# First chunk's loads moved ahead of a branch, weights regrouped on the queue, and one head's mask moved to VectorE, in a kernel of banded attention and two MLPs

## The chip, the cores and the metric

The program runs on one core of a Trainium2 chip. The metric is the device time of one execution in microseconds; for the kernel before it is the median of three runs. A core has TensorE (PE in the rows, with its weight loads as PEld), VectorE (DVE), ScalarE (ACT), GpSimd (POOL) and SyncE (SP), which here issues transfers; each engine takes its instructions in order from its own queue.

## The reference

Attention with sink keys and a window, for 2 batches, 8 heads, 768 positions and 64 columns a head, and then two MLPs on the 1,536 tokens:

```python
scores = q @ k.transpose(0, 1, 3, 2) / sqrt(64)
rel = pos[:, None] - pos[None, :]
keep = (pos[None, :] < n_sink) | ((rel >= 0) & (rel < window))   # 4 sinks, window 128
a = exp(where(keep, scores, -1e9) - rowmax)
attn = (a / (a.sum(-1) + 1e-9)) @ v
x = attn as [1536, 512]
h = x @ w_in;   x = (h - tanh(h)) @ w_out                        # 512 -> 2048 -> 512
h = x @ w_in2;  x = (h * clip(h + 3, 0, 6) / 6) @ w_out2
```

`n_sink`, `window` are 64-bit integers in memory, and the MLPs' weights reach the chip as 64-bit floats.

## The kernel before

**Tiles.** The tokens are cut into three chunks of 512 (`CHUNKS`), each four blocks of 128 queries. The heads are taken in four pairs. For a chunk c and a pair m the attention consists of these steps: `begin` loads the pair's queries and keys (tile `qk`, two transfers a run of blocks, one for each head) and its values (tile `v`, two transfers); `score` (L447) runs for each of the four blocks, for both heads: matmul into a bank `ps_a`, on VectorE a predicated copy (L469) that puts the block's own diagonal half over the earlier one, then one operation that masks, scales and takes the minimum (L471), and on ScalarE an exponential with its sum (L475). `soft` (L479) normalises on VectorE (L492). `turn_sink` and `turn_p` (L504) transpose the probabilities on TensorE; for each head of the pair ScalarE copies them to `p` (L513) and GpSimd makes two masked copies of them, with `affine_select`, one for the block's own keys and one for the keys of the block before (L517, L521). `mix` (L526) multiplies with the values, and splits the result into a high part `xh` (ScalarE, L547) and a low part `xl` (VectorE, L548), the inputs of the MLP.

**The MLP** has 64 groups a chunk (`GROUPS`), each of 12 matmuls of 128x512: every product is done as three (high by high, high by low, low by high: L175, L176, L177). Two groups share one weight tile of 128x1024, called a pair p of groups; 32 weights make the two MLPs. In the first chunk each weight is decoded from its 64-bit form: `w_load` (SP, tile `raw`, 1 MB, four buffers), `w_sign` (ScalarE, two operations, L127 and L129, tile `r`, two buffers), `w_scale` (ScalarE, L107, tile `dec`), `w_exponent` (VectorE, L118), `w_round` (VectorE, L135), `w_keep` (SP, stores the decoded weight for later chunks), and `w_split` into high `wh` (ScalarE for the weights 0 and 1, L151; GpSimd for the others, L149) and low `wl` (VectorE, L152). `w_step(p, half)` calls these for weights up to six ahead of p. The later chunks load the kept weights, and their attention runs between the groups of the chunk before.

**Order.** A few loads, the masks and the test of `n_sink` and `window` (DMA of the two scalars, `scalars_value`, `is_band`) stand ahead of a branch; the banded case is the one that runs. Behind the branch a planner orders the instructions of each engine by a simulated timeline; within what the data allows it may place a later one first. `keep_in_program_order` pins an instruction behind the one before it on its engine; that is done for the loads and the scalings of the weights 0 to 5. `startup` (L779) lists the attention of chunk 0 and drops the twelve calls of `w_step` for p from -6 to -1 into it; the factor 1.25 decides where:

```python
while warm and left < 1.25 * len(warm):
    mlp.w_step(*warm.pop(0))
```

With 41 operations in the list, the first of the twelve calls comes when 14 are left, and the first scaling behind `mix` of pair 1. Ahead of the branch only pair 0 of chunk 0 is loaded, on SP. The tile `vsk` of sink values is set to zero by GpSimd behind the branch (L415), and eight small transfers (`sinks`, L443) follow on SP.

## Time and profile before

| | |
|---|---|
| time of the runs | 671.25 us (671.24, 671.25, 672.27) |
| time of the profiled execution | 676.76 us |
| its span | 675.0 us |
| TensorE busy | 647.0 us, 96% of the span |
| VectorE, ScalarE, GpSimd busy | 394.4, 365.7, 103.8 us |
| mean granted clock of TensorE | 0.978 |
| moved by DMA | 98.87 MB |

Busy shares count the time in which an engine has an instruction under way; matmuls overlap, so that a busy TensorE need not be at its peak pace. The granted clock is a share of 2.4 GHz: 1.00 is the upper level and 0.50 the lower. Times within the execution count from the start of the span. Line numbers are those of the kernel before.

### The profile page before, as it was taken

The numbers are of one execution on the slowest core, as the hardware profiler recorded it, in microseconds if no ns is written. First come the engines' busy times: TensorE is split into PE (matmuls) and PEld (weight loads), VectorE is DVE, ScalarE is ACT, GpSimd is POOL, SyncE is SP. The second block draws the span as 40 slices with busy tenths as digits, with TensorE's granted clock in tenths as the row PEclk, the third lists the DMA queues.
The fourth block names the chain that finished last, engine by engine and source line by source line (L and its number), as shares of the span: only waits on it lengthen the run. The fifth ranks groups of instructions, "written<-read, shape, count | busy, mean of one in ns | idle before, by whom it ended". The sixth has DMA issues, their size and how long they took to land.

```text
span 675.0 us, 8142 instructions
## 1 busy us (share of the span) xinstructions
PE 647.0 (96%) x2924; PEld 494.7 (73%) x2924; DVE 394.4 (58%) x711; ACT 365.7 (54%) x614; POOL 103.8 (15%) x114
## 2 busy tenths in 40 slices
PE   3897899999999999999999999999999999999995
PEld 2555677777777787887776777778788888888884
DVE  4659599887797754365555465444355444455431
ACT  3769779887978633354444454444354443454421
POOL 1234122234452421000102020201000000000000
PEclk9959699999999999999999999999999999999999
DMA  5969879968668731423314221113133323221001
GB/s 104 324 168 340 306 292 312 319 248 304 224 216 293 227 113 33 135 104 125 103 63 125 91 95 63 62 63 126 62 126 124 102 86 115 73 70 55 0 1 67
DMA packets 38896, 98.87 MB, mean 146 GB/s; under 512 B 17856, under 2 KB 25024, under 8 KB 30656
## 3 DMA queue, kind: packets, MB, share of 16 engines
q1 hardware_dynamic: 38848, 98.27, 44.3%
q8 instruction: 25, 0.41, 0.2%
q14 instruction: 23, 0.19, 0.1%
HBM read 78.33 MB, written 19.92 MB: 146 GB/s over the span
## 4 chain that ended last, share of the span: by engine, by line
PE 90%; ACT 2%; DVE 2%; DMA 2%; SPq 2%; POOL 1%; issue 1%; POOLq 0%; DVEq 0%; ACTq 0%
PE ps_h L175 13%; PE ps_y L175 13%; PE ps_h L176 13%; PE ps_h L177 13%; PE ps_y L176 13%; PE ps_y L177 13%; PE ps_a L463 5%; PE ps_a L543 4%; PE ps_a L511 1%; DMA raw<-in_w_dram 1%; SPq L282 1%; ACT r L127 1%; ACT r L129 1%; DVE dec L118 1%; DMA raw<-in_window_dram 1%
## 5 line engine op out<-in xcount | busy, mean ns | idle before, releaser
L176 PE MATMUL ps_y<-gl,wh 128*128 128x512 f32 x384 | 151.0, 394 | 0.0
L177 PE MATMUL ps_y<-gh,wl 128*128 128x512 f32 x384 | 150.0, 391 | 0.0
L175 PE MATMUL ps_y<-gh,wh 128*128 128x512 f32 x384 | 143.9, 400 | 0.0
L152 DVE TENSOR_TENSOR wl<-raw,wh 128x1024 fp32r<-128x1024 f32 x64 | 79.3, 1239 | 58.2 <-ACT wh L151 57.3
L151 ACT CAST wh<-raw 128x1024 fp32r<-128x1024 f32 x64 | 67.2, 1050 | 48.6 <-PE ps_y L176 40.9
L175 PEld LDWEIGHTS ps_y<-gh,wh 128*128 128x128 f32 x384 | 71.7, 188 | 22.0 <-issue 5.9
L176 PEld LDWEIGHTS ps_y<-gl,wh 128*128 128x128 f32 x384 | 72.1, 188 | 16.6 <-issue 1.9
L177 PEld LDWEIGHTS ps_y<-gh,wl 128*128 128x128 f32 x384 | 72.1, 188 | 15.6 <-issue 0.3
L175 PE MATMUL ps_h<-xh,wh 128*128 128x512 f32 x192 | 77.8, 409 | 1.2 <-ACT xh L547 1.2
L177 PE MATMUL ps_h<-xh,wl 128*128 128x512 f32 x192 | 77.2, 402 | 0.6 <-DVE wl L152 0.6
L176 PE MATMUL ps_h<-xl,wh 128*128 128x512 f32 x192 | 77.1, 402 | 0.0
L175 PE MATMUL ps_h<-yh,wh 128*128 128x512 f32 x192 | 76.6, 402 | 0.0
L176 PE MATMUL ps_h<-yl,wh 128*128 128x512 f32 x192 | 76.2, 397 | 0.0
L177 PE MATMUL ps_h<-yh,wl 128*128 128x512 f32 x192 | 76.0, 396 | 0.0
L233 ACT ACTIVATE th<-ps_h,three 128x512 f32<-128x512 f32 x48 | 32.8, 686 | 70.1 <-PE ps_h L177 69.9
L235 DVE SCALAR_TENSOR_TENSOR th<-th,ps_h 128x512 f32<-128x512 f32 x48 | 32.8, 684 | 53.3 <-ACT th L233 53.1
L463 PE MATMUL ps_a<-qk 64*128 64x264 f32 (+1 forms) x192 | 48.4, 477 | 11.4 <-DVE keep L709 6.8
L475 ACT ACTIVATE sc<-sc,mn 128x132 f32<-128x132 f32 x96 | 38.3, 401 | 37.1 <-DVE mn L471 36.9
L149 POOL CAST wh<-dec 128x1024 fp32r<-128x1024 f32 x30 | 37.5, 1250 | 114.6 <-PE ps_y L176 68.1
L227 ACT ACTIVATE th<-ps_h 128x512 f32<-128x512 f32 x48 | 28.6, 597 | 48.9 <-PE ps_h L177 39.4
L229 DVE TENSOR_TENSOR th<-ps_h,th 128x512 f32<-128x512 f32 x48 | 32.9, 686 | 36.2 <-ACT th L227 36.2
L463 PEld LDWEIGHTS ps_a<-qk 64*128 64x128 f32 x192 | 23.6, 220 | 32.6 <-issue 20.6
(74 smaller groups left out, 903.8 us busy)
## 6 DMA issues: line engine op xcount, KB each, us to landing
raw<-in_w_dram SPq DMA_DIRECT2D x32, 1024.0 KB
raw<-keep SPq DMA_DIRECT2D x32, 1024.0 KB
keep<-dec SPq DMA_DIRECT2D x32, 512.0 KB
out_dram<-ob SPq DMA_DIRECT2D x12, 256.0 KB
qk<-in_qkv_dram SPq DMA_DIRECT2D x8, 325.0 KB
qk<-in_qkv_dram SPq DMA_DIRECT2D x8, 260.0 KB
qk<-in_qkv_dram SPq DMA_DIRECT2D x8, 195.0 KB
v<-in_qkv_dram SPq DMA_DIRECT2D x8, 160.0 KB
```

The costliest lines, as they stand in the source:

```text
L149: nc.gpsimd.tensor_copy(out=wh, in_=src)
L151: nc.scalar.copy(out=wh, in_=src)
L152: nc.vector.tensor_sub(out=wl, in0=src, in1=wh.bitcast(F32))
L175: mm(out=ps, lhsT=wh, rhs=ah, start=first, stop=False)
L176: mm(out=ps, lhsT=wh, rhs=al, start=False, stop=False)
L177: mm(out=ps, lhsT=wl, rhs=ah, start=False, stop=last)
L227: nc.scalar.activation(out=th, in_=ps, func=ACTF.Tanh)
L229: nc.vector.tensor_sub(out=u, in0=ps, in1=th)
L233: nc.scalar.activation(out=th, in_=ps, func=ACTF.Relu, bias=self.three)
L235: nc.vector.scalar_tensor_tensor(out=u, in0=th, scalar=6.0, in1=ps, op0=ALU.min, op1=ALU.mult)
L463: nc.tensor.matmul(out=ps[:, 0:w], lhsT=qk[:, e, 0:128], rhs=qk[:, first:e + 1, 128:KEYS], start=True, stop=True)
L475: nc.scalar.activation(out=sc, in_=sc, func=ACTF.Exp, scale=-1.0, bias=mn, accum_out=s["sm"][:, a, i:i + 1])
```

## The change

- The queries and keys of the pairs 0 to 2 of chunk 0 are loaded ahead of the branch by SP, and the values of all four pairs by ScalarE's queue. The buffers for them are fixed tiles (three for `qk`, used in turn by m; four for `v`, one for each m) that the later chunks use too. Pair 3's queries and keys go into the tile of pair 0, once its scores are done; `begin` of pair 3 stands at tick 4 instead of 6.
- In the list of `startup`, `w_load(0)` comes right behind `begin` of pair 0, and `w_load(1)` to `w_load(3)` directly behind `begin` of pair 3, pinned in that order. `w_load` does nothing for a weight already loaded.
- The factor 1.25 becomes 0.8: the first of the twelve calls comes when nine operations are left, and the first scaling behind the last `score` of pair 3.
- For the second head of a pair in chunk 0, VectorE makes the two masked copies directly out of the PSUM bank, by multiplying with masks of zeros and ones; ScalarE's copy and GpSimd's two selections of that head go. Two more mask tiles are made for it ahead of the branch.
- GpSimd clears `vsk` ahead of the branch. The high parts of the weights 0 and 1 are made by GpSimd, as those of the others.
- The other arm of the branch, which does not run here, takes its room from the same tiles.

```diff
@@ -83,7 +83,7 @@
     def w_load(self, p):
-        if p >= self.n_pairs:
+        if p >= self.n_pairs or p in self.raw:
             return
         nc = self.nc
         if p < PAIRS:
@@ -145,7 +145,7 @@
         src = self.dec.pop(p).bitcast(F32) if p < PAIRS else self.raw.pop(p)
         wh = self.spl_p.tile([128, 1024], F32R, tag="wh", name="wh")
         wl = self.spl_p.tile([128, 1024], F32R, tag="wl", name="wl")
-        if 2 <= p < PAIRS:
+        if p < PAIRS:
             nc.gpsimd.tensor_copy(out=wh, in_=src)
         else:
             nc.scalar.copy(out=wh, in_=src)
@@ -268,25 +268,28 @@
     return out
-def load_pair(nc, qk_p, v_p, qkv, m, rs):
-
-    n = sum(r[3] for r in rs)
-    qk = qk_p.tile([128, n, KEYS], F32, tag="qk", name="qk")
-    v = v_p.tile([128, 2, n, 64], F32, tag="v", name="v")
+def pair_buffers(pool, pairs, n):
+
+    qk = [pool.tile([128, n, KEYS], F32, tag=f"qk{m}", name="qk") for m in range(pairs - 1)]
+    v = [pool.tile([128, 2, n, 64], F32, tag=f"v{m}", name="v") for m in range(pairs)]
+    return qk, v
+
+
+def load_qk(dma, qk, qkv, m, rs):
     for i, b, j, k in rs:
         for a in range(2):
             h = slice(64 * a, 64 * (a + 1))
-            nc.sync.dma_start(out=qk[h, i:i + k, :], in_=qkv[b, 2 * m + a, h, j:j + k, 0:KEYS])
+            dma(out=qk[h, i:i + k, :], in_=qkv[b, 2 * m + a, h, j:j + k, 0:KEYS])
+
+
+def load_v(dma, v, qkv, m, rs):
     for i, b, j, k in rs:
         for a in range(2):
-            nc.sync.dma_start(out=v[:, a, i:i + k, :], in_=qkv[b, 2 * m + a, :, j:j + k, KEYS:BLOCK])
-    return qk, v
-
-
-def load_blocks(nc, pool, qkv, h, runs, first=0, last=BLOCK, tag="raw"):
-    n = sum(r[3] for r in runs)
-    t = pool.tile([128, n, last - first], F32, tag=tag, name=tag)
-    for i, b, j, m in runs:
+            dma(out=v[:, a, i:i + k, :], in_=qkv[b, 2 * m + a, :, j:j + k, KEYS:BLOCK])
+
+
+def load_blocks(nc, t, qkv, h, rs, first, last):
+    for i, b, j, m in rs:
         nc.sync.dma_start(out=t[:, i:i + m, :], in_=qkv[b, h, :, j:j + m, first:last])
     return t
@@ -399,20 +402,19 @@
-    def __init__(self, ctx, tc, qkv, vs, ready, masks, ident, mlp):
+    def __init__(self, ctx, tc, qkv, vs, ready, vsk, masks, ident, mlp):
         self.tc, self.nc = tc, tc.nc
         _, self.H, _, self.NB, _ = qkv.shape
         self.mlp, self.qkv, self.vs, self.ident = mlp, qkv, vs, ident
         self.ready = ready
-        self.own_keep, self.mask = masks
+        self.own_keep, self.mask, self.own, self.prev = masks
         pool = lambda nm, n: ctx.enter_context(tc.tile_pool(name="at_" + nm, bufs=n))
-        self.qk_p, self.v_p, self.s_p = pool("qk", 2), pool("v", 3), pool("s", 2)
+        self.s_p = pool("s", 2)
         self.p_p, self.px_p = pool("p", 2), pool("px", 4)
         self.scale = -1.0 / 64.0 ** 0.5
         self.wide = True
         self.st = {}
-        self.vsk = pool("const", 1).tile([32, self.H // 2, 4, 128], F32, name="vsk")
-        self.nc.gpsimd.memset(self.vsk, 0.0)
+        self.vsk = vsk
     def bank(self, kind):
@@ -429,10 +431,12 @@
         qb = self.query_blocks(c)
         kb = ([(qb[0][0], qb[0][1] - 1)] if qb[0][1] > 0 else []) + qb
         s = self.st[it] = dict(qb=qb, kb=kb)
-        if it == (0, 0):
-            s["qk"], s["v"] = self.ready
-        else:
-            s["qk"], s["v"] = load_pair(self.nc, self.qk_p, self.v_p, self.qkv, m, runs(kb))
+        qk, v = self.ready
+        s["qk"], s["v"] = qk[m % len(qk)], v[m]
+        if c > 0 or m >= len(qk):
+            load_qk(self.nc.sync.dma_start, s["qk"], self.qkv, m, runs(kb))
+        if c > 0:
+            load_v(self.nc.sync.dma_start, s["v"], self.qkv, m, runs(kb))
     def sinks(self, c):
@@ -509,10 +513,17 @@
         pt = self.bank("p")
         for i in range(nq):
             nc.tensor.transpose(pt[:, 128 * i:128 * (i + 1)], s["sc"][:, a, i, 0:128], self.ident)
+        px = self.px_p.tile([128, nq, 2, 128], F32, tag="px", name="px")
+        s["px", a] = px.rearrange("p j t s -> p (j t s)")
+        if self.wide and a == 1:
+            src = pt[:, 0:128 * nq].rearrange("p (j s) -> p j s", s=128)
+            for t, keep in ((1, self.own), (0, self.prev)):
+                nc.vector.tensor_tensor(
+                    out=px[:, :, t, :], in0=src, in1=keep.unsqueeze(1).to_broadcast([128, nq, 128]), op=ALU.mult
+                )
+            return
         p = self.p_p.tile([128, 128 * nq], F32, tag="p", name="p")
         nc.scalar.copy(out=p, in_=pt[:, 0:128 * nq])
-        px = self.px_p.tile([128, nq, 2, 128], F32, tag="px", name="px")
-        s["px", a] = px.rearrange("p j t s -> p (j t s)")
         src = p.rearrange("p (j s) -> p j s", s=128)
         nc.gpsimd.affine_select(
             out=px[:, :, 1, :], in_=src, pattern=[[0, nq], [1, 128]], compare_op=ALU.is_ge,
@@ -554,7 +565,8 @@
         for m in range(self.H // 2):
             it = (c, m)
             at = lambda k, *p: out[2 * m + k].append(p)
-            at(0, self.begin, it)
+
+            out[4 if it == (0, 3) else 2 * m].append((self.begin, it))
             if m == 0:
                 at(1, self.sinks, c)
             for i in range(n):
...
...
@@ -699,8 +715,8 @@
         for c in range(NSINK):
             nc.vector.memset(self.is_sink[:, c:c + 1], float(c))
         self.keep = [tile_(f"keep{j}", SLOT) for j in range(3)]
-        self.wm, self.far = tile_("wm", 1), tile_("far", 128)
-        self.own_keep = tile_("own_keep", 128, I32)
+        self.wm, self.far = tile_("wm", 1), self.keep[2][:, 0:128]
+        self.own_keep = di
     def finish(self, n_sink, window):
         nc, delta, is_sink = self.nc, self.delta, self.is_sink
@@ -718,7 +734,10 @@
         big = 8.0 * BIG
         for keep in self.keep:
             nc.vector.tensor_scalar(out=keep, in0=keep, scalar1=big, scalar2=-big, op0=ALU.mult, op1=ALU.add)
-        return self.own_keep, self.keep
+        own, prev = self.delta, self.past
+        nc.vector.tensor_scalar(out=prev, in0=delta, scalar1=0.0, scalar2=None, op0=ALU.is_gt)
+        nc.vector.tensor_scalar(out=own, in0=delta, scalar1=0.0, scalar2=None, op0=ALU.is_le)
+        return self.own_keep, self.keep, own, prev
 def when(t, n):
@@ -744,13 +763,20 @@
     kf = GROUPS // 4
     glob = ctx.enter_context(tc.tile_pool(name="glob", bufs=1))
     raw = scalars(tc, glob, n_sink, window)
-    ready = load_pair(nc, glob, glob, qkv, 0, [(0, 0, 0, CHUNKS[0] // 128)])
+    vsk_room = glob.tile([128, kd * 4 * 128], F32, name="vsk")
+    vsk = vsk_room[0:32].rearrange("p (m i d) -> p m i d", m=kd, i=4)
+    nc.gpsimd.memset(vsk, 0.0)
+    ready = pair_buffers(glob, kd, 5)
+    for m, qk in enumerate(ready[0]):
+        load_qk(nc.sync.dma_start, qk, qkv, m, [(0, 0, 0, CHUNKS[0] // 128)])
     ident = glob.tile([128, 128], F32, name="ident")
     make_identity(nc, ident)
     masks = Masks(tc, glob)
     warm = glob.tile([128, 1], F32, name="warm")
     nc.vector.memset(warm, 0.0)
     nc.scalar.activation(out=warm, in_=warm, func=ACTF.Exp)
+    for m, v in enumerate(ready[1]):
+        load_v(nc.scalar.dma_start, v, qkv, m, [(0, 0, 0, CHUNKS[0] // 128)])
     ns, win = scalars_value(tc, glob, raw)
     flag = is_band(tc, glob, ns, win)
     kept = masks.finish(ns, win)
@@ -758,12 +784,15 @@
     with tc.If(band != 0) as cmp:
         with ExitStack() as arm:
             mlp = Mlp(arm, tc, w64, out, CHUNKS, kd, kf)
-            at = BandAttention(arm, tc, qkv, vs, ready, kept, ident, mlp)
+            at = BandAttention(arm, tc, qkv, vs, ready, vsk, kept, ident, mlp)
             banded(mlp, at)
     with cmp.Else():
         with ExitStack() as arm:
             mlp = Mlp(arm, tc, w64, out, CHUNKS, kd, kf, ahead=3)
-            at = DenseAttention(arm, tc, qkv, ident, ns, win, mlp)
+
+            flat = [t.rearrange("p j c -> p (j c)") for t in ready[0]]
+            room = [*flat, ready[1][0].rearrange("p a j c -> p (a j c)"), vsk_room, flat[0]]
+            at = DenseAttention(arm, tc, qkv, room, ident, ns, win, mlp)
             dense(mlp, at)
@@ -778,11 +807,13 @@
 def startup(mlp, at):
     first = [p for t in at.ticks(0) for p in t]
+    for n in range(4):
+        first.insert(1 if n == 0 else first.index((at.begin, (0, 3))) + n, (mlp.w_load, n))
     warm = [(p, h) for p in range(-6, 0) for h in range(2)]
     for n, p in enumerate(first):
         p[0](*p[1:])
         left = len(first) - 1 - n
-        while warm and left < 1.25 * len(warm):
+        while warm and left < 0.8 * len(warm):
             mlp.w_step(*warm.pop(0))
```

## Rows read from the trace of the kernel before

**Rows 1.** Page, part 2: busy tenths and granted clock in 40 slices.
```profile
PE   3897899999999999999999999999999999999995
...
PEclk9959699999999999999999999999999999999999
```

**Rows 2.** Windows by stage: busy us of PE, PEld, DVE, ACT, POOL; clock, DMA.
```profile
25.95:55.00 29.05, 25.47 (x115) 15.68 (x114) 18.24 (x57) 23.64 (x48) 6.77 (x11) 0.71 0.78 246
55.00:72.95 17.95, 12.34 (x57) 7.78 (x56) 14.52 (x16) 13.97 (x19) 8.93 (x7) 0.86 0.95 329
72.95:81.40 8.45, 8.45 (x26) 6.75 (x27) 3.83 (x6) 6.64 (x8) 1.04 (x1) 0.70 0.89 300
81.40:668.00 586.60, 585.91 (x2667) 454.26 (x2665) 343.41 (x557) 310.82 (x500) 81.09 (x83) 1.00 0.40 133
```

**Rows 3.** Groups, 0 to 82 us: busy us, mean ns, idle before.
```profile
L129 ACT ACTIVATE r<-raw 128x1024 f16<-128x1024 f32 x9 | 12.1, 1355 | 0.0
...
L135 DVE CUSTOM_DVE_ANT_0 dec<-dec,r 128x2048 uint16<-128x2048 uint16 x8 | 11.3, 1417 | 0.4 <-ACT r L129 0.4
...
L107 ACT ACTIVATE dec<-raw 128x1024 f32<-128x1024 f32 x9 | 10.0, 1141 | 2.4 <-DMA keep<-dec 1.5 <-DVE wl L152 0.9
...
L176 PE MATMUL ps_h<-xl,wh 128*128 128x512 f32 x21 | 9.5, 451 | 0.0
...
L521 POOL TENSOR_SCALAR_AFFINE_SELECT px<-p 128x512 f32<-128x512 f32 x8 | 7.5, 935 | 0.0
...
L152 DVE TENSOR_TENSOR wl<-dec,wh 128x1024 fp32r<-128x1024 f32 x5 | 7.4, 1472 | 0.3 <-ACT wh L151 0.3
...
L118 DVE TENSOR_SCALAR dec<-dec 128x1024 int32<-128x1024 int32 x8 | 5.7, 710 | 1.7 <-ACT dec L107 1.7
...
L548 DVE TENSOR_TENSOR xl<-ps_a,xh 128x512 fp32r<-128x512 f32 x4 | 2.7, 686 | 3.4 <-ACT xh L547 3.4
```

**Rows 4.** Chain of waits of 0 to 82 us: start, length, what.
```profile
19.07 6.86 DMA raw<-in_w_dram
...
25.95 1.19 ACT r L127
...
69.03 3.26 PE ps_a L543 x13
...
81.13 0.23 PE ps_h L175
```

**Rows 5.** Timeline of VectorE and ScalarE: start, length, instruction, idle before it.
```profile
6.20 0.28 DVE L713 TENSOR_SCALAR far<-delta,wm 128x128 f32<-128x128 f32 x1
...
6.85 1.63 DVE L711 CAST own_keep<-keep 128x128 int32<-128x128 f32 x1
...
9.66 0.30 DVE L471 CUSTOM_DVE_ANT_0 sc<-ps_a,keep 128x132 f32<-128x132 f32 x1
...
13.49 0.08 DVE L471 DVE_READ_ACCUMULATOR2_ANT mn<- 128x1 f32 x1
...
15.93 0.30 DVE L471 CUSTOM_DVE_ANT_0 sc<-ps_a,keep 128x132 f32<-128x132 f32 x1 [2.36 <-PE ps_a L463]
...
18.48 1.34 DVE L492 TENSOR_TENSOR sc<-sc,rs 128x512 f32<-128x512 f32 x2
...
55.01 0.39 ACT L475 ACTIVATE sc<-sc,mn 128x132 f32<-128x132 f32 x1
```

**Rows 6.** Timeline of SP's queue: start, time spent issuing, transfers.
```profile
8.42 2.70 SPq L443 DMA_DIRECT2D vsk<-in_vs_dram  x8
...
12.49 1.16 SPq L282 DMA_DIRECT2D v<-in_qkv_dram  x2
```

**Rows 7.** Windows: the first loads, and a stage without late data.
```profile
3.00:6.76 3.76, 0.00 (x0) 0.03 (x1) 1.66 (x12) 0.00 (x0) 0.16 (x1) 1.00 0.85 171
...
18.05:28.62 10.57, 10.57 (x65) 7.48 (x61) 8.30 (x44) 7.58 (x24) 3.31 (x6) 1.00 1.09 328
```

**Rows 8.** Windows, all engines: early in the unbroken stream.
```profile
80.00:120.00 40.00, 40.00 (x170) 29.97 (x169) 37.82 (x61) 34.60 (x54) 8.45 (x7) 1.00 0.87 315
```

More of the change, by code (lines that the diff above doesn't have):

```diff
@@ L573, with __init__ @@
     BUFS = dict(t=1, v=1, s=1)
-    def __init__(self, ctx, tc, qkv, ident, n_sink, window, mlp):
+    def __init__(self, ctx, tc, qkv, room, ident, n_sink, window, mlp):
         super().__init__(ctx, tc, qkv, ident, mlp)
-        self.raw_p = ctx.enter_context(tc.tile_pool(name="at_raw", bufs=1))
         nc, const, S = self.nc, self.const, self.S
+        self.raws = room[3:6]
         self.n_sink = n_sink
-        ki = const.tile([128, S], I32, name="ki")
+        ki, self.kpos, self.rel = (t[:, 0:S] for t in room[0:3])
+        ki = ki.bitcast(I32)
         nc.gpsimd.iota(ki, pattern=[[1, S]], base=0, channel_multiplier=0)
-        self.kpos = const.tile([128, S], F32, name="kpos")
         nc.vector.tensor_copy(out=self.kpos, in_=ki)
         nc.gpsimd.iota(ki, pattern=[[-1, S]], base=0, channel_multiplier=1)
-        self.rel = const.tile([128, S], F32, name="rel")
         nc.vector.tensor_copy(out=self.rel, in_=ki)
@@ L598, in head @@
         s = self.st[it] = dict(h=h, qb=qb, kb=[(b, j) for b in bs for j in range(NB)])
-        s["qr"] = load_blocks(nc, self.raw_p, self.qkv, h, runs(qb), 0, 128, "rawq")
-        kv = load_blocks(nc, self.raw_p, self.qkv, h, runs(s["kb"]), 128, BLOCK)
-        s["kr"], s["vr"] = kv[:, :, 0:SLOT], kv[:, :, SLOT:SLOT + 64]
+        nq, nk = len(qb), len(s["kb"])
+        q, k, v = (
+            t[:, 0:n * w].rearrange("p (j c) -> p j c", c=w)
+            for t, n, w in zip(self.raws, (nq, nk, nk), (128, SLOT, 64))
+        )
+        s["qr"] = load_blocks(nc, q, self.qkv, h, runs(qb), 0, 128)
+        s["kr"] = load_blocks(nc, k, self.qkv, h, runs(s["kb"]), 128, KEYS)
+        s["vr"] = load_blocks(nc, v, self.qkv, h, runs(s["kb"]), KEYS, BLOCK)
         self.split(it, 128)
```

## The prediction

> **What bounds the kernel now.** I read the page first, then the stages, the chain of waits, and the queues. The slices [rows 1] show TensorE full from about 80 us to the end; only the first five slices have gaps and a low granted clock. The stages [rows 2] say it exactly: from 81.40 to 668 us TensorE is busy 585.91 of 586.60 us at clock 1.00, so there nothing but less TensorE work would help, and the change removes none. Before that, TensorE waits for the first chunk's attention. So the question is only how early the unbroken MLP stream can begin.
>
> I measure that with one number, the **zero point**: the time from which all MLP matmuls would have had to run back to back to stand where they stand. By 82 us 21 + 21 + 20 matmuls into ps_h and 3 into ps_y have run (65; the group of L176 stands in [rows 3]). At full clock one takes 0.23 us of the chain [rows 4] (0.232 by the starts of two that lie twelve apart, 78.17 and 80.96). 65 x 0.232 = 15.1 us, so the zero point is 82 - 15.1 = 66.9 us. What the change gains is 66.9 less the new zero point, less any new stall afterwards.
>
> What made it 66.9? In the chain [rows 4] the weights are issued at 19.07 and the first lands 6.86 us later; ScalarE's decoding starts on that landing; much later the last pair's output matmuls run from 69.03 for 3.26 us (the granted clock is 0.86 and 0.70 around them [rows 2], a mixture of the 2.4 and 1.2 GHz levels), then the copy of the output, then the MLP at 72.95. In between, from 25.95 to 55 us, ScalarE is busy 23.64 of 29.05 us and VectorE 18.24 [rows 2]: attention of pairs 2 and 3 and decoding of weights share both in-order queues, and an exponential of pair 3's scores still runs at 55.01 [rows 5].
>
> **The change, part by part.** All terms are built forward to E, the time at which the last pair's attention output is split.
>
> Masks and memset. VectorE starts the scores at 9.66 [rows 5]. Its cast at L711 took 1.63 us beside GpSimd's memset of vsk, the next one as long, both ended at 8.48; L713, a like one without the memset beside it, took 0.28 [rows 5]. With the memset moved ahead, about 1.2 us goes; the two new mask tiles cost 0.28 each at most. Scores start near 9.0 us. Cover: before, the keys of pair 0 were there by 7.73; if the added traffic delays them past 9.0 the gain of 0.7 is lost and up to 2 us more.
>
> Loads ahead of the branch. Pair 1's keys came late: VectorE stood idle 2.36 us before 15.93 [rows 5] and again before the next score. Issued before the branch they are due about 9 us earlier, so I remove both waits. VectorE's price of a pair is then: eight scores from 9.66 to 13.57, 3.9 us [rows 5]; normalising 1.7 (0.37 for the reciprocal and 1.34 [rows 5]); the low half of the output 0.69 [rows 3]; and new, two masks from PSUM, which I price as L548, the nearest operation of 128x512 with PSUM as source: 2 x 0.69 = 1.4. Together 7.7 us. Four pairs take 30.8 us, of which 3.8 come after the last score: the last score would end at 9.0 + 27.0 = 36.0. A stage without late data took longer than its prices: from 18.05 to 28.62 [rows 7] VectorE did 12 scores and two normalisings, 9.3 us by these prices, in 10.6. With that factor, 1.14, the last score ends at 39.8.
>
> Mask on VectorE. It takes one ScalarE copy (0.56) and two GpSimd selections off each pair; these took 0.94 us each at L521 [rows 3], up to 1.6 when VectorE was busy beside them. The last pair's chain of four selections before 69.03 shrinks to two: 2 to 3 us. VectorE pays 1.4 a pair, already counted.
>
> Decoding later. The calls of the warm-up now start nine operations before the end instead of fourteen. The scaling step is pinned behind what ScalarE was given before it; it now comes after the last score of pair 3, and the exponent, rounding and split follow it. So VectorE does no decoding before the last score; that is how scores ending at 55 us become scores ending near 40. The sign step is not pinned: its two buffers let the planner place two of them (2.5 us each: 1.19 for L127 [rows 4] and 1.36 for L129 [rows 3]) among the exponentials. ScalarE's own work for a pair is about 4.6 us (eight exponentials at 0.39 [rows 5], copies 0.24, 0.56, 0.57) against VectorE's 7.7, so the 5 us partly hide: bounds 0 and 5, I take 2.
>
> First weight. It is issued at the branch, near 7 us, not at 19.07, ahead of the eight small vsk transfers (8.42, 2.70 us [rows 6]). But 3 x 520 KB of keys and 4 x 256 KB of values are under way (sizes from the tiles): 2.6 MB, at the 171 GB/s of the first loads [rows 7] 15 us, so until about 18. The weight lands between 14 (7 + the 6.86 of before) and 24 us (all of it first, then its own share). An early sign step in ScalarE's in-order queue would wait for it, with exponentials behind, and VectorE's normalising behind those. Bounds 0 and 6, I take 3.
>
> One rule of the Trainium skill speaks against the second queue. Two value transfers cost SP 1.16 us of issuing [rows 6], so eight on ScalarE's queue take some 4.6 us off SP, on an engine that has nothing to do before 10 us. The Trainium skill, DMA: Bandwidth & Descriptors, section Issuing engines are not separate DMA queues, says that transfers of several engines run on the same 16 DMA engines and interleave, so only issue time is saved. By that rule the values on the second queue would hold the first weight back to the far bound, 6 us for this term and 664 us in the end; with no sharing it would be 0 and 658. All loads of before went through SP, so no row here shows two queues at once.
>
> Tail. After the last score: normalising 1.7, sinks and transposes 1.5 to 1.9, copy 0.56, two selections 1.3 to 1.9, output matmuls 1.73 to 3.26, copy 0.59: 7.4 to 9.9, I take 8.5; scaling steps of decoding in between on ScalarE (1.14 each [rows 3]), I take 1. So E = 39.8 + 2 + 3 + 8.5 + 1 = 54.3 us.
>
> From E to the zero point. A low clock costs at the start: 26 matmuls took 8.45 us instead of 6.0 [rows 2], 2.4 us lost; I keep it (bound below 0). Less is done ahead than before, as decoding is later; the first weight can be ready about 5.5 us after its scaling (0.71 + 1.42 + a GpSimd copy of 1.0 to 2.0 + 1.47 [rows 3]), so about 12 matmuls, 2.8 us. New zero point 54.3 + 2.4 - 2.8 = 53.9; gain 13.0.
>
> Then the lead is smaller: before, four weights were split when the stream began. Now one or two. A pair of groups takes TensorE 5.6 us (24 x 0.232); VectorE needs 0.71 + 1.42 + 1.47 for a weight and 1.37 for gating, 5.0 us. That is enough, barely; I charge 3 us (bounds 0 and 6). The split of weights 0 and 1 goes from ScalarE (1.05 us each at L151) to GpSimd, which has time; covered by the above. The later chunks keep their TensorE bound; the values have four buffers instead of three and the keys three instead of two, so I cost this at nothing; the cover is the 585.91 of 586.60, and where SP stood still on them it would cost a weight load.
>
> Sum: 13.0 - 3 = 10.0 us. The profiled execution took 676.76 us with a span of 675.0; the runs' median is 671.25. The start-up does not depend on that difference, so I subtract from the median: 671.25 - 10.0 = 661.2.
>
> **The rivals.** *Clean start-up.* None of the waits appears: last score 36, tail 8, clock stays up, no lag: E = 44 to 47, zero point 45 or so with less work ahead, less 2 of lag: gain about 19, 652 us. For it: ScalarE has slack. Against: no stage of before ran without gaps.
> *ScalarE waits for the weight.* The planner places a sign step by its own due times, and the first weight lands behind all 2.6 MB at 24 us: the full 6 us instead of 3, and 2 us more at the second weight; E = 59.3, gain 5, 666 us. For it: the first sign step of before began on the very landing of its weight, 25.95 [rows 4]. Against: later in the stream there is slack. The rule of the DMA page named above makes this case likelier.
> *The loads were hidden anyway.* Transfers and decoding fill 50 us whatever their order, E near 64 plus lag: 671 us. For it: DMA share 0.95 from 55 to 72.95 [rows 2].
> *Slower: decoding starves the stream.* With decoding begun after the scores, VectorE has not the pace: from 80 to 120 us it was busy 37.82 of 40 us [rows 8] while TensorE was full. If stretched operations take a pair from 5.0 to 6.2 us, 0.6 us over TensorE's pace, the first chunk's 32 pairs lose up to 19 us, less the 13 gained: 677 us. It decides from about 6.0 us a pair. Against: from 25.95 to 72.95 us VectorE was busy 32.8 of 47.0 us [rows 2], so it can catch up.
>
> **How the numbers follow.** Forecast 0.45, clean start 0.20, ScalarE's wait 0.18, hidden anyway 0.06, starved 0.11. A measurement of this kernel tells 0.2% (1.3 us) from no change. Faster 0.83, same 0.06, slower 0.11. The range from 651 to 671.5 leaves out most of the starved case and the best of the clean one; the likeliest alone spans 656 to 666.
>
> **What would show it.** Right: scores of pair 3 end near 40 to 46 us; no wait of TensorE for keys; the first weight lands between 14 and 24; unbroken MLP from about 55; after that the same matmul pace to the end. Wrong: a wait of ScalarE for raw of over 6 us, decoding still among the exponentials, gaps of TensorE behind wl between 55 and 150 us, or the VectorE masks later than GpSimd's selections.

## The result and the profile after

The change made the kernel slower: 679.05 us (677.20 to 679.77, four runs) against 671.30 us beside it, a ratio of 1.0108 with an interval of 1.0086 to 1.0130. The forecast was 661.2 us and faster.

The profiled execution of after took 677.20 us with a span of 675.4. That of before on which the forecast rests was longer than its own median (676.76 against 671.25). A second profile of the kernel before (span 670.0, 671.77 us) shows where: MLP matmul number 96 started at 85.38 us instead of 89.97, and from there both run alike. What differs most ahead of it is TensorE's clock: in two stretches the granted clock was 0.87 and 1.00 (the upper level throughout) where the first profile had 0.71 and 0.70, mixtures of the two levels [rows 2], and 35 matmuls instead of 26 fell into the second of them:

```profile
25.95:55.00 29.05, 21.68 (x116) 13.00 (x114) 19.19 (x58) 24.34 (x51) 8.63 (x11) 0.87 0.82 254
...
72.95:81.40 8.45, 8.05 (x35) 6.45 (x35) 7.05 (x10) 7.49 (x10) 0.07 (x1) 1.00 0.91 304
```

Page of after, part 2 (answers to [rows 1]):

```profile
PE   2488999999899999999999999999999999999995
...
PEclk9987999999999999999999999999999999999999
```

Windows of after, the stages of [rows 2 and 8] and one later stretch; columns as there:

```profile
25.95:55.00 29.05, 21.77 (x144) 15.00 (x144) 22.72 (x89) 19.72 (x65) 6.31 (x10) 0.94 0.83 226
55.00:72.95 17.95, 16.98 (x70) 12.53 (x71) 17.92 (x17) 16.48 (x18) 10.81 (x7) 0.81 0.97 330
72.95:81.40 8.45, 8.05 (x35) 5.99 (x34) 8.11 (x12) 8.29 (x10) 1.36 (x1) 1.00 1.05 401
81.40:668.00 586.60, 583.58 (x2651) 451.34 (x2649) 346.00 (x552) 311.03 (x500) 83.48 (x83) 1.00 0.39 133
80.00:120.00 40.00, 40.00 (x173) 30.39 (x172) 39.08 (x62) 36.80 (x54) 9.83 (x9) 1.00 1.00 366
130.00:180.00 50.00, 46.98 (x210) 33.26 (x211) 40.66 (x72) 38.97 (x68) 17.83 (x16) 1.00 0.72 250
```

The same stretch, 130 to 180 us, in the second profile of before:

```profile
130.00:180.00 50.00, 49.70 (x236) 36.76 (x236) 38.88 (x76) 41.75 (x71) 18.81 (x17) 1.00 0.74 258
```

The reader sees two losses. TensorE's first two slices went from 3 and 8 tenths to 2 and 4: the start-up is emptier, not fuller. And from 130 to 180 us, where before had no gap to speak of, TensorE stands still for 3 us. From 55 to 81 us VectorE has hardly any idle time left (17.92 of 17.95, 8.11 of 8.45).

Where the time lies is told by the starts of the MLP's matmuls, read from the traces and numbered from 0 (E, to which the sum was built, is read as the start of the last pair's `xh`):

| matmul | before, profile | before again | after | sign pinned | values later | both |
|---|---|---|---|---|---|---|
| this execution (median of the runs) | 676.76 (671.30) | 671.77 (671.93) | 677.20 (679.05) | 674.60 (672.61) | 673.57 (672.73) | 664.54 (665.17) |
| E | 72.31 | 69.40 | 66.34 | 53.29 | 66.06 | 46.03 |
| MLP matmuls started before E | 36 | 36 | 18 | 1 | 18 | 1 |
| 0 | 49.49 | 45.47 | 57.91 | 52.99 | 57.62 | 45.69 |
| 96 | 89.97 | 85.38 | 85.54 | 80.58 | 87.35 | 76.02 |
| 264 | 135.35 | 130.76 | 130.82 | 127.52 | 131.91 | 121.17 |
| 408 | 179.29 | 174.73 | 179.82 | 175.36 | 176.86 | 167.83 |
| 2303 (last) | 667.20 | 662.63 | 667.66 | 663.22 | 664.70 | 655.68 |

(The last three columns are experiments, below.) After is level with the second profile of before up to number 264, so the start-up gained nothing: E came 3.1 us earlier, but 18 fewer MLP matmuls (4.2 us at 0.232) stood before it. Between 264 and 408 after loses 5.1 us (49.0 against 44.0); from 408 to the end all take 487.8 to 487.9 us. The profiled execution of after was the fastest of its four runs, so the two traces show 5.0 of the 7.75 us between the medians; where the rest lies they do not show.

Why the start-up gained nothing is in three views. First the queues of after that issue transfers (answers to [rows 6]; SPq is SP's, ACTq ScalarE's; start, time spent issuing):

```profile
1.72 9.47 SPq L282 DMA_DIRECT2D qk<-in_qkv_dram  x6
13.72 0.34 SPq L91 DMA_DIRECT2D raw<-in_w_dram  x1
14.32 8.49 SPq L447 DMA_DIRECT2D vsk<-in_vs_dram  x8
...
24.28 1.54 SPq L91 DMA_DIRECT2D raw<-in_w_dram  x3
...
3.48 8.45 ACTq L288 DMA_DIRECT2D v<-in_qkv_dram  x4
```

Second the timeline of VectorE and ScalarE (answers to [rows 5]; in brackets the idle time before and what ended it):

```profile
8.10 0.22 DVE L727 CAST di<-keep 128x128 int32<-128x128 f32 x1
...
10.22 0.30 DVE L475 CUSTOM_DVE_ANT_0 sc<-ps_a,keep 128x132 f32<-128x132 f32 x1 [0.57 <-PE ps_a L467]
...
12.43 0.29 DVE L475 CUSTOM_DVE_ANT_0 sc<-ps_a,keep 128x132 f32<-128x132 f32 x1 [1.91 <-PE ps_a L467]
...
26.45 0.17 DVE L488 TENSOR_SCALAR rs<-sm 128x8 f32<-128x8 f32 x1 [8.31 <-ACT sc L479]
...
52.82 1.28 DVE L118 TENSOR_SCALAR dec<-dec 128x1024 int32<-128x1024 int32 x2
54.03 1.21 DVE L135 CUSTOM_DVE_ANT_0 dec<-dec,r 128x2048 uint16<-128x2048 uint16 x1
55.16 0.68 DVE L118 TENSOR_SCALAR dec<-dec 128x1024 int32<-128x1024 int32 x1
55.76 2.05 DVE L135 CUSTOM_DVE_ANT_0 dec<-dec,r 128x2048 uint16<-128x2048 uint16 x1
57.74 1.12 DVE L118 TENSOR_SCALAR dec<-dec 128x1024 int32<-128x1024 int32 x1
...
59.38 0.68 DVE L521 TENSOR_TENSOR px<-ps_a,delta 128x512 f32<-128x512 f32 x1
...
12.67 0.40 ACT L479 ACTIVATE sc<-sc,mn 128x132 f32<-128x132 f32 x1 [9.88 <-DMA v<-in_qkv_dram]
...
22.57 1.12 ACT L127 ACTIVATE r<-raw 128x1024 int32<-128x1024 uint32 x1 [7.98 <-DMA raw<-in_w_dram]
```

Third the chain of waits of 0 to 82 us (answers to [rows 4]):

```profile
13.72 8.82 DMA raw<-in_w_dram
...
24.28 7.50 DMA raw<-in_w_dram
31.80 1.13 ACT r L127
...
59.38 1.27 DVE px L521 x2
```

What they show: the keys' issuing took SP until 11.2 us, so that the first weight went out at 13.72 and landed at 22.54 (13.72 + 8.82). ScalarE, held by issuing values, did its first exponential at 12.67 (10.16 in the second profile of before), then three more, and then came the sign step of weight 0, for which it waited 7.98 us. Everything behind it in its queue waited too, and VectorE's normalising behind that, 8.31 us. At the other end, after the last exponential at 50.59, VectorE put six decoding operations (52.82 to 58.8) ahead of the last pair's masks at 59.38.

### The profile page after: what moved, and what is told of

Read it like the earlier page. It is cut to its first block, busy times and chain, and to the rows that moved or that the text cites. A ratio compares the mean times of both kernels' runs of the same rounds, so it can differ in the third digit from the quotient of the medians.

```text
span 675.4 us, 8172 instructions
## 1 busy us (share of the span) xinstructions
PE 637.6 (94%) x2924; PEld 490.3 (73%) x2924; DVE 403.0 (60%) x721; ACT 362.5 (54%) x608; POOL 104.6 (15%) x108
## 4 chain that ended last, share of the span: by engine, by line
PE 74%; DVE 10%; DMA 5%; ACT 5%; issue 2%; SPq 0%; POOL 0%; ACTq 0%; DVEq 0%
PE ps_y L175 11%; PE ps_h L175 11%; PE ps_h L176 11%; PE ps_h L177 11%; PE ps_y L176 11%; PE ps_y L177 11%; DMA raw<-in_w_dram 4%; PE ps_a L554 3%; DVE dec L135 3%; PE ps_a L467 3%; DVE dec L118 2%; DMA keep<-dec 2%; DVE wl L152 2%; ACT r L127 2%; ACT dec L107 1%
## 5 line engine op out<-in xcount | busy, mean ns | idle before, releaser
L176 PEld LDWEIGHTS ps_y<-gl,wh 128*128 128x128 f32 x384 | 72.1, 188 | 17.3 <-issue 2.6
L149 POOL CAST wh<-dec 128x1024 fp32r<-128x1024 f32 x32 | 44.5, 1393 | 92.7 <-PE ps_y L176 60.2
L467 PE MATMUL ps_a<-qk 64*128 64x264 f32 (+1 forms) x192 | 44.6, 453 | 13.5 <-DVE delta L739 9.4
L127 ACT ACTIVATE r<-raw 128x1024 int32<-128x1024 uint32 x32 | 36.8, 1151 | 24.7 <-DVE dec L135 15.2
```

What stands on the lines that cost most here:

```text
L127: self.nc.scalar.activation(out=r, in_=raw[:, :, 0].bitcast(U32), func=ACTF.Copy, scale=2.0 ** -29)
L149: nc.gpsimd.tensor_copy(out=wh, in_=src)
L176: mm(out=ps, lhsT=wh, rhs=al, start=False, stop=False)
L467: nc.tensor.matmul(out=ps[:, 0:w], lhsT=qk[:, e, 0:128], rhs=qk[:, first:e + 1, 128:KEYS], start=True, stop=True)
```

## The experiments

Each run's time is a median of several rounds, with the kernel before timed beside it (671.91, 672.23, 672.14 and 672.18 us in the four batches); the second number is its ratio to that, with the 95% interval. The theories were: the **decoding** (VectorE's pace once decoding starts later, the rival "decoding starves the stream"), the **early sign step** (ScalarE waits for the weight), and the **crowded transfers** (all loads of chunk 0 at once). The expectations stand as they were written before each run. In them A and D are the decoding, B is the crowded transfers, and W (W1, W2) is the wait for the weight and what brings it about; beside the kernel before, W says that the attention sets the time.

**The kernel before, again.** No edit; 671.93 us, 0.9997 (0.9966 to 1.0027).

> The kernel before, unchanged, for a second profile: the first one's execution took 676.76 us where the runs took 671.3. All theories: 671 us in the runs. If the typical execution differs in the start-up, this profile shows the zero point near 61 us instead of 66.9 and a span near 669.5; if it differs in the middle, the zero point is again near 67 and some stretch after 82 us is shorter.

**The mask put back on GpSimd.** 678.52 us, 1.0094 (1.0060 to 1.0128): no recovery, so VectorE's added 1.4 us a pair isn't by itself what costs.

```diff
-        if self.wide and a == 1:
+        if False:
```

> The kernel after with the second head's mask back on ScalarE and GpSimd. Theory A (VectorE's work up to about 170 us sets the pace, and the masks and the later decoding add to it): VectorE gets back 5 us, the time falls by 2 to 5 us, to 674 to 677. Theory B (the bytes of the early loads delay the weights, and all else follows): no change within 1 us, 678 to 680.

**Decoding early again.** 677.61 us, 1.0077 (1.0042 to 1.0111): 1.4 us, inside the intervals. So neither part of the decoding's load costs by itself. Yet the traces of this run and the one above differ from after: matmuls 264 to 408 took 43.8 and 43.6 us, so that the loss of 5.1 us is gone there, but number 264 started at 136.47 and 139.82 us instead of 130.82. The time is lost earlier instead; in these two executions the mean granted clock was 0.974, in that of after 0.990, so part of this can be the clock.

```diff
-        while warm and left < 0.8 * len(warm):
+        while warm and left < 1.25 * len(warm):
```

> The kernel after with the factor of the start-up list back at 1.25. Theory A: decoding starts earlier in VectorE's stream, the time falls by 3 to 6 us, to 673 to 676. Theory B: ScalarE waits for the same late weights, no change within 1 us.

**The loads put back.** Pair 0 alone ahead of the branch, all on SP; the rest of the change stays. 678.21 us, 1.0092 (1.0053 to 1.0131). I had expected the crowd to be the cause by itself; it is not. Here the first weight is issued at 7.14 us, and the sign step, again behind the fourth exponential, begins at 12.01 us after a wait of only 1.14.

```profile
12.01 1.12 ACT L127 ACTIVATE r<-raw 128x1024 int32<-128x1024 uint32 x1 [1.14 <-DMA raw<-in_w_dram]
```

```diff
-        if c > 0 or m >= len(qk):
+        if c > 0 or m > 0:
...
-        if c > 0:
+        if c > 0 or m > 0:
...
-    for m, v in enumerate(ready[1]):
-        load_v(nc.scalar.dma_start, v, qkv, m, [(0, 0, 0, CHUNKS[0] // 128)])
+    for m, v in enumerate(ready[1][:1]):
+        load_v(nc.sync.dma_start, v, qkv, m, [(0, 0, 0, CHUNKS[0] // 128)])
```

> The kernel after with only pair 0 loaded ahead of the branch, on SP, and the pairs 1 to 3 behind the branch, on SP, as before (buffers, the order of the weights and the rest as in the kernel after). Theory A: the scores of pair 1 come later by about 4 us and decoding with them, 679 to 683. Theory B: the first weight lands no later than 26 us without holding up ScalarE among the first exponentials, the time falls by 4 to 8 us, to 671 to 675.

**The sign step pinned.** After, with the first sign operation of the weights 0 to 5 kept behind what ScalarE was given before it (its scaling, and so the last score). 672.61 us, 1.0017 (0.9998 to 1.0036): 6.4 us back.

```diff
-        self.nc.scalar.activation(out=r, in_=raw[:, :, 0].bitcast(U32), func=ACTF.Copy, scale=2.0 ** -29)
+        ins = self.nc.scalar.activation(out=r, in_=raw[:, :, 0].bitcast(U32), func=ACTF.Copy, scale=2.0 ** -29)
+        if p < 6:
+            self.tc.keep_in_program_order(ins)
```

> The kernel after with the first operation of each sign step of the weights 0 to 5 pinned in program order, so that none stands among the first exponentials. Theory W (ScalarE's wait of 8 us for the first weight holds up the attention, and that is the loss): VectorE's idle time of 8.3 us behind 18 us goes, the stream begins 6 to 8 us earlier, 670 to 674. Theory D (the weights' decoding runs at VectorE's and ScalarE's pace up to about 170 us and decides when the first chunk ends, wherever the attention stands): 676 to 680, the matmul 408 of the MLP again near 180 us.

**The values later.** After, with the keys ahead of the branch but of the values only pair 0's, on SP; those of pairs 1 to 3 in `begin`. 672.73 us, 1.0002 (0.9975 to 1.0029): 6.3 us back.

```diff
-        if c > 0:
+        if c > 0 or m > 0:
...
-    for m, v in enumerate(ready[1]):
-        load_v(nc.scalar.dma_start, v, qkv, m, [(0, 0, 0, CHUNKS[0] // 128)])
+    for m, v in enumerate(ready[1][:1]):
+        load_v(nc.sync.dma_start, v, qkv, m, [(0, 0, 0, CHUNKS[0] // 128)])
```

> The kernel after with the values of the pairs 1 to 3 loaded by SP behind the branch and behind the first weight, only pair 0's ahead of it on SP; keys as in the kernel after. Theory W (with the 256-byte pieces of the values as the reason for the late landing): SP's six key transfers issue in 4 us instead of 9.5, the first weight lands near 16 instead of 22.5, 672 to 675. Theory D: 676 to 680.

SP's queue in this run:

```profile
1.72 4.02 SPq L282 DMA_DIRECT2D qk<-in_qkv_dram  x6
...
8.08 0.34 SPq L91 DMA_DIRECT2D raw<-in_w_dram  x1
8.61 7.66 SPq L447 DMA_DIRECT2D vsk<-in_vs_dram  x8
```

The same six key transfers are issued in 4.02 us instead of 9.47, and the weight goes out at 8.08 instead of 13.72. ScalarE still waits 5.2 us for it.

**Single parts on the kernel before.** Its mask on VectorE: 672.55 us, 0.9996 (0.9975 to 1.0016). Its factor 0.8 instead of 1.25: 668.75 us, 0.9955 (0.9934 to 0.9977). Both: 669.72 us, 0.9955 (0.9935 to 0.9974). Factor 0.8 with the sign pinned: 669.32 us, 0.9956 (0.9929 to 0.9984). So decoding later is worth 3.4 us by itself, the mask nothing here, and the pin nothing where the first weight is issued at 19.3 us as before and the sign step begins near 26 us: what is harmful is the sign step in after's order of loads, not the sign step as such.

> The kernel before with the second head's mask of the first chunk on VectorE, nothing else. Theory W: the last pair's chain of selections is shorter, 669 to 672. Theory D: VectorE gets 5 us more work before 72 us, some of it in idle time: 671 to 675.

> The kernel before with the factor of the start-up list at 0.8, nothing else: decoding later. Theory W: later decoding leaves ScalarE free for the exponentials, 664 to 670. Theory D: decoding starts about 5 us later and stays late, 674 to 678.

> The kernel before with the factor 0.8 and the mask on VectorE, loads as before. The factor alone gave 668.75 us, the mask alone 672.55. Theory W: the mask shortens the end of the attention, which now is what the stream waits for, 666 to 669. Theory D (VectorE's decoding sets the pace): 5 us more for VectorE, 669 to 673.

> The kernel before with the factor 0.8 and the sign steps of the weights 0 to 5 pinned. Theory W: ScalarE is free of decoding among the exponentials, the wait of 1.9 us goes, 665 to 668. Theory D: two sign steps (5 us of ScalarE) move into the busy stretch behind the scores and decoding falls behind, 669 to 674.

**The weights' order undone.** After without the inserted loads of the weights 0 to 3. 676.80 us, 1.0067 (1.0041 to 1.0093): 2.2 us back, though the intervals touch. The weight then goes out at 22.24 us, and ScalarE's sign step, now behind the thirteenth exponential, still waits 7.1 us for it. So the weight's early place in the list moves the sign step, but isn't the main loss.

```diff
-    for n in range(4):
-        first.insert(1 if n == 0 else first.index((at.begin, (0, 3))) + n, (mlp.w_load, n))
```

> The kernel after without the four weight loads in the start-up list (the weights are loaded where the warm-up calls ask for them, as before); loads ahead on two queues, mask and factor 0.8 as in the kernel after. Theory W1 (the early place of the first load makes the planner put its sign step behind the fourth exponential, long before the bytes land): the sign step stands behind the fourteenth, ScalarE waits under 3 us, 668 to 673. Theory W2 (the two crowded queues alone are the loss, whatever the place): the six keys again issue in 9.5 us, the first weight lands at 26 us or later, 675 to 679.

**Sign pinned and values later together.** The two edits above in one kernel: 665.17 us (663.70 to 666.69), 0.9896 (0.9869 to 0.9924). 13.9 us less than after, where the single ones gave 6.4 and 6.3; it beats both kernels, and it is faster than either expectation said.

> The kernel after with both remedies: sign steps pinned, and the values of the pairs 1 to 3 behind the first weight on SP. Each alone gave 672.6 and 672.7 us. Theory W1: with the sign step pinned nothing waits for the first weight early on, so the second remedy adds only what the queues give, 670 to 672. Theory W2: the keys, the small transfers and weights all come earlier, 666 to 670.

The timeline of its VectorE at the end of the last pair:

```profile
37.34 1.34 DVE L498 TENSOR_TENSOR sc<-sc,rs 128x512 f32<-128x512 f32 x2
38.60 1.28 DVE L118 TENSOR_SCALAR dec<-dec 128x1024 int32<-128x1024 int32 x2
39.80 0.68 DVE L523 TENSOR_TENSOR px<-ps_a,delta 128x512 f32<-128x512 f32 x1
```

Here only two exponent steps come between normalising and the masks, where after put six decoding operations. The last exponential runs at 36.36 us instead of 50.59, the last `xh` at 46.03 instead of 66.34.

**One queue.** After with all eight value transfers on SP behind the keys: same bytes ahead of the weight, no second queue. 680.50 us, 1.0114 (1.0079 to 1.0149).

```diff
-        load_v(nc.scalar.dma_start, v, qkv, m, [(0, 0, 0, CHUNKS[0] // 128)])
+        load_v(nc.sync.dma_start, v, qkv, m, [(0, 0, 0, CHUNKS[0] // 128)])
```

> All eight value transfers stay ahead of the branch, but on SP's queue behind the six key transfers; bytes and their place before the first weight are as in the changed kernel. If it is the second queue that harms (issuing of keys and values stretched by each other, ScalarE held by issuing): the six key transfers are issued in about 4 us again, the first exponential comes near 10 us, and the time falls to that of the run with the values later, 671 to 674.5. If it is the bytes ahead of the weight: the first weight still lands after 21 us and the time stays at 677 to 680.

Its queue and ScalarE's timeline:

```profile
1.71 4.01 SPq L282 DMA_DIRECT2D qk<-in_qkv_dram  x6
5.77 8.11 SPq L288 DMA_DIRECT2D v<-in_qkv_dram  x8
14.97 0.34 SPq L91 DMA_DIRECT2D raw<-in_w_dram  x1
...
9.04 0.40 ACT L479 ACTIVATE sc<-sc,mn 128x132 f32<-128x132 f32 x1 [6.74 <-DVE mn L475]
...
19.76 1.12 ACT L127 ACTIVATE r<-raw 128x1024 int32<-128x1024 uint32 x1 [8.97 <-DMA raw<-in_w_dram]
```

The keys are issued in 4 us and the first exponential comes at 9.04, 3.6 us earlier than in after; yet the weight goes out at 14.97, the sign step waits 8.97 us, and nothing is gained. So what costs is the eight value transfers ahead of the weight, whatever queue they are on; whether it is by their bytes or by the time that SP is held issuing them is not separated. My expectation that the second queue would show as such was wrong, and the other one missed too: the weight landed at 19.8 us, not after 21, and the time came out above 680.

**The loads back and the sign pinned.** 668.96 us, 0.9937 (0.9914 to 0.9960), 9.2 us less than with the loads back alone: there too the early sign step was what cost, and more than I had expected. It waited for raw less than in after (6.8 us in all up to 75 us, against 9.5), and yet the pin gives more: the last exponential moves from 45.41 to 41.58 us, the last `xh` from 65.83 to 51.71, so that 10.3 of these 14.1 us lie behind the last exponential. The wait for the weight is therefore not the whole price of the early sign step. The distance to 665.17 is what having the keys of pairs 1 and 2 ahead of the branch is worth, 3.8 us (intervals touch).

> Pairs 1 to 3 are loaded in begin again, and the sign step is pinned as well. If the early sign step is what kept the run with the loads put back at 678 us, pinning it gives about the 6 us that it gave in the changed kernel: 671 to 673.5. Rival: the first weight, issued ahead of the keys of pair 1, makes those keys late whatever ScalarE does, and the time stays above 675.

**What the two other parts are worth in the best version.** With the mask back on GpSimd 668.99 us, 0.9946 (0.9928 to 0.9964); with the factor 1.25 668.24 us, 0.9928 (0.9899 to 0.9957). Against 665.17 the mask is worth 3.8 us (intervals apart) and the later decoding about 3.1 (intervals touch).

> The version with the sign step pinned and the values later (665.2 us), with the mask back on GpSimd. If the mask on VectorE is neutral, as it was beside the kernel before and within the changed kernel: 664 to 667. Rival: with the waits on weight and values gone, GpSimd's four selections are in the last pair's chain again, and it is slower by the 2 to 3 us that the prediction gave them: 667.5 or more.

> The same version with the factor 1.25 instead of 0.8. If decoding later is worth what it gave the kernel before (3.4 us), 667.5 to 670. Rival: with the sign step pinned, the smaller factor only makes the weights late (the 5 us that the stream lost between 130 and 180 us), and the earlier calls give 664 or less.

Windows of the best version, and of the same without the mask:

```profile
75.00:130.00 55.00, 55.00 (x236) 40.79 (x235) 54.97 (x87) 51.34 (x77) 18.46 (x14) 1.00 1.00 363
```

```profile
75.00:130.00 55.00, 52.83 (x216) 37.80 (x216) 52.43 (x81) 50.75 (x73) 17.68 (x13) 1.00 0.92 336
```

The last `xh` starts only 0.85 us later without the mask (46.88 against 46.03); most of the rest is lost after 75 us, where TensorE stands still for 2.2 us. The prediction had looked for the 2 to 3 us in the last pair's chain. Why GpSimd's selections cost that much later was not tried.

## Why the prediction was wrong

**The sum against the profile.** The forecast took 10 us off; the profiled executions say +0.46 us (667.66 against 667.20 for the last matmul). The 10.5 us between are in two places, the zero point and the stream behind it, below. A third step is not of the change: "the start-up does not depend on that difference, so I subtract from the median". The 4.6 us by which the profiled execution of before was longer lie in that very start-up (number 96 at 89.97 against 85.38, with the lower granted clock shown above). The gain of 13.0 us had been worked out from a start-up that the median run doesn't have.

**Zero point.** Forecast 53.9. By the same measure, matmul 96 at 85.54 less 96 x 0.232 = 22.3, it came to 63.3, against 67.7 for the profiled before: a gain of 4.4 us instead of 13.0. E was to be 54.3; the last pair's `xh` began at 66.34. The 12 us split at the last exponential, forecast at 44.8 (39.8 + 2 + 3) and found at 50.59: 5.8 us ahead of it and 6.2 behind.

**First weight: the step that failed first.** The text had it issued "near 7 us" and let ScalarE wait 3 us, bounds 0 and 6. It landed at 22.54, inside the 14 to 24 given; but it went out at 13.72, behind the keys, whose issuing ended at 11.2, and ScalarE's waits for raw sum to 9.5 us, beyond the bound. What I missed was its place: a load listed earlier made the planner put the sign step behind the fourth exponential of the kernel, so that it did not come "later in the stream", where "there is slack": half of pair 0 and all later scores stood behind it. Waits of after, 0 to 75 us (total, times, longest):

```profile
DVE rs L488 <- ACT sc L479: 12.8, 4, 8.3
...
ACT sc L479 <- DMA v<-in_qkv_dram: 9.9, 1, 9.9
ACT r L127 <- DMA raw<-in_w_dram: 9.5, 2, 8.0
```

The rival "ScalarE waits for the weight" had the mechanism and its sign, with 666 us too small a price. The pin shows the cost on the chip: 6.4 us in after, 7.6 with the values later (672.73 to 665.17), 9.2 with the loads back, none on the kernel before with the factor 0.8. How it divides between the wait and the tail was not measured by a run of its own; with the loads back most of it lies in the tail. Three of the signs of being wrong that were put down came true in after: this wait of over 6 us, decoding among the exponentials (sign steps from 22.57 us on), and VectorE's masks, ending at 60.7 us, behind GpSimd's selections, ending at 59.4.

**Tail.** Forecast 8.5 + 1. In the three pinned versions with the factor 0.8 and VectorE's mask the last `xh` comes 9.7 to 10.1 us after the last exponential, as forecast; in after 15.75. By the traces the reason is the same early sign step: weights 0 and 1 being ready, the planner put their rounding on VectorE ahead of the last pair's masks. "VectorE does no decoding before the last score" held, but the tail was not protected.

**From E to the zero point: the step that failed behind it.** The sum lets the zero point follow E at -0.4 us (2.4 for the low clock, less 2.8 for about 12 matmuls done ahead). With the sign pinned E was met: 53.29 against the forecast 54.3. Yet the runs took 672.61 us, not 661.2. One MLP matmul stood before E, and by the measure above the zero point was 58.3, 5.0 us behind E; in the best version it was 7.7 us behind (53.8 against 46.03). The trace of the pinned version shows what held the stream back: TensorE's matmuls start 0.43 us apart from 53.58 to 61.5 us, behind a stretch with gaps (the granted clock from 55 to 64 us is 0.62, mostly the lower level), and it waits for the low half of the weights (50 to 96 us; total, times, longest):

```profile
PE ps_h L179 <- DVE wl L154: 3.1, 2, 1.6
```

In the best version these waits sum to 4.4 us. So an earlier E is worth less than its distance, since the decoding was put behind it. Four kernels, each by one profile, show it together: with E at 46.88 (best without the mask), 51.71 (loads back, pinned), 55.22 (best with the factor 1.25) and 61.23 us (before with 0.8) the runs took 668.99, 668.96, 668.24 and 668.75 us.

**Loads ahead of the branch.** Right for the keys, and worth 3.8 us. Wrong for the values, most of which nothing needed so early: ahead of the branch they cost 6.3 to 7.4 us (672.61 to 665.17 with the sign pinned). On the second queue they also made the pair 0 keys and the scalars late (VectorE's second score waited 1.91 us); on SP's queue neither was late, and the time was no better. With both causes gone the last exponential ran at 36.36 us; the case without gaps said 36.0 for the last score and the forecast 39.8, so the prices were sound and the factor of 1.14 was not needed there.

**The second queue.** The runs show that it saved nothing: with the values on SP the time is 680.5 against 679.05, inside the intervals. The Trainium skill, DMA: Bandwidth & Descriptors, section Issuing engines are not separate DMA queues, says that transfers of several engines interleave on the same 16 DMA engines; these two times agree with that, though no row shows the sharing itself. The rule pointed at the right term and the right side; the 664 us was still far off, since the price of a late weight was. In one thing the rows differ: that section of the Trainium skill grants the second engine a saving of issue time, and here the keys' issuing on SP rose from 4.02 to 9.47 us.

**Masks and memset.** Right: the cast took 0.22 us instead of 1.63; scores began at 10.22 instead of 9.0 only for the late loads, and the first exponential came at 9.04 to 9.06 where the issuing of the keys was not stretched. **Mask on VectorE.** Priced at 0.69 us an operation; the groups of 0 to 82 us (answers to [rows 3]) show 0.68:

```profile
L135 DVE CUSTOM_DVE_ANT_0 dec<-dec,r 128x2048 uint16<-128x2048 uint16 x8 | 12.5, 1559 | 0.0
...
L118 DVE TENSOR_SCALAR dec<-dec 128x1024 int32<-128x1024 int32 x8 | 6.7, 844 | 0.4 <-ACT dec L107 0.3
...
L521 DVE TENSOR_TENSOR px<-ps_a,delta 128x512 f32<-128x512 f32 x4 | 2.7, 681 | 0.0
```

**Decoding later, and the lead.** Right in direction (3.4 us on the kernel before). The charge of 3 us, bounds 0 and 6, was 5.1 between matmuls 264 and 408. The groups above show longer operations already before 82 us (1559 and 844 ns, 1417 and 710 in [rows 3]). In the later stretch, the chain of waits of 128 to 182 us runs in after through the decoding (rounding 17.3%, scaling 12.0%, exponent 12.0% of it), in both profiles of before mostly through TensorE's own matmuls. So the rival "decoding starves the stream" came true in part, and its 677 us lies nearest to the result, but as a cause it is 2.1 us over the charge; mask and factor undone took the loss away there and did not bring the time back. Which part of the change makes the decoding late there, and why the best version loses 2.7 us too (46.7 against 44.0), stays open.

## What to carry to other kernels

Loading something earlier can move its consumer earlier too: where a planner orders in-order engines, look for the instruction that a new early transfer makes eligible, and pin it behind the work that must not wait. Load ahead only what is needed next, in the order of need; a second queue doesn't make room for the rest. Before counting a gain in full, ask whether what comes next is ready for it: with the sign pinned E came 13 us earlier than in after and matmul 96 only 5. And work out a gain in a start-up from an execution whose start-up is the typical one.

## What was not expected of the hardware

The time that a queue spends issuing is not a property of the transfer. From the first to the last, six key transfers took 4.02 us alone and 9.47 beside eight value transfers from ScalarE; the single issues last 0.59 to 0.74 us in both, the rest is time between them (none goes out from 4.54 to 9.28 us). Eight small `vsk` transfers took 2.70 us [rows 6] and 4.50 to 8.49 behind a weight of 1 MB; with the weights' order undone no weight stood ahead of them, only keys and values, and they took 7.04. On one queue it begins within a run of like transfers: the first three values go out 0.65 and 0.62 us apart (5.77, 6.42, 7.04), the next ones at 8.12, 10.43 and 12.15, the last two 0.6 us apart again. An engine that computes as well is held by this: ScalarE's first exponential moved from 9.06 to 12.67 us, though the minimum that it needed was there at 10.52.

Parts of a change don't add up singly: the mask was worth 0 on the kernel before and within after, and 3.8 us once the other waits were gone, while the two harmful parts did add (6.4 + 6.3 against 13.9).
